# A decode kernel on one core: the key scores of two heads computed by one matmul, with a 4-byte instead of an 8-byte step of the moving operand

## The chip, the cores and the metric

The kernel runs on one core of one Trainium2 chip. The metric is device time in microseconds (us). "Span" is the time from the first to the last instruction of a profiled execution; it is about 1.5 to 3 us shorter than the time of the run. PE is the tensor engine, PEld its weight loads, DVE the vector engine, ACT the scalar engine, and SPq the queue that issues the DMAs.

## The reference, cut to what matters

One token attends to a window of 4096 cached keys in each head. A small dense GELU branch runs beside it, and a gate mixes the two.

```python
Hq, Hkv, Sk, Dh = 32, 16, 32768, 128;  W = 4096;  D = 576;  F = 4608
q = (x @ wq).reshape(B, 1, Hq, Dh).transpose(0, 2, 1, 3)
k = repeat(k_cache[:, :, Sk - W:, :], 2, axis=1)      # 2 query heads per key head
v = repeat(v_cache[:, :, Sk - W:, :], 2, axis=1)
p = softmax(q @ k.T * Dh ** -0.5)
a = (p @ v).reshape(B, 1, Hq * Dh) @ wo
b = gelu(x @ w1 + b1) @ w2 + b2
g = sigmoid((x * gate_w).sum(-1)); return g * a + (1 - g) * b
```

The kernel loads 53.6 MB: 16.8 MB of keys, 16.8 MB of values, and weights. Each byte is used once.

## The kernel before: the parts that matter

The load goes through four large buffers, A to D, which are used again and again. Its order is: w1 (B), wq (A), key tiles 0 to 3 (C, D, B, A), half of w2 (B), value tiles 0 to 3 (C, D, A, C), wo (D), and the rest of w2. So value tile 3 needs the buffer that value tile 0 gives up. That happens only after the softmax and after the matmuls of value tile 0.

A key transfer holds two heads `b` in alternating partitions. The vector engine transposes it as 4-byte words, each word a pair of bf16 (2294 ns for 128 x 2048 words). In the result `kt` the keys of the two heads alternate (`b`), and each word holds two head dimensions (`t`). A score matmul reads one head and one of the two dimensions, so its consecutive columns lie 4 bf16, or 8 bytes, apart (a bank is a piece of 512 fp32 columns of a PSUM tile):

```python
    s_ps = ps_s.tile([P, NCK * 8], FP32, name="s_ps")            # two PSUM banks
    ...
            kv = kt[:].rearrange("p (c e k b t) -> p c e k b t", e=2, b=2, k=16, t=2)
            for u in range(2):
                for b in range(2):
                    for j in range(4):
                        h = h0 + b
                        nc.tensor.matmul(
                            s_ps[:, u * 512 : (u + 1) * 512].rearrange("p (c k) -> p c k", k=16),
                            lhsT=qz[:, h, j, :],
                            rhs=kv[:, u * SL // 2 : (u + 1) * SL // 2, j // 2, :, b, j % 2],
                            ...)
    nc.vector.reduce_max(out=m1[:], in_=s_ps[:], axis=AX.X)
    ...                                       # 8 exps from s_ps (ACT), 2 transposes of p (DVE), sums
    for g in range(NG):
        v_t = big.tile([P, NCK, Dh], BF16, name="v_t", tag="CDAC"[g])
        load(v_t, A_v_cache, g, v_cuts[g])
        ...                                   # 128 matmuls into o_ps
    ...                                       # y_ps += rows of wo and w2, both halves of y in one bank
    out_row = const.tile([64, DH], BF16, name="out_row")
    nc.vector.tensor_copy(out=out_row[0:33, :], in_=y_ps[0:33, :])
    nc.sync.dma_start(out=..., in_=out_row[0:64:32, :])          # two rows
```

## Time and profile before

| | before |
|---|---|
| time, median of 3 runs | 145.44 us (145.25 to 145.54) |
| span | 143.9 us |
| busy: PE / DVE / ACT | 102.9 / 56.5 / 11.9 us |
| DMA, mean over the span | 374 GB/s |

First the strips of the kernel before. Each digit is the busy share, in tenths, of one fortieth of the span (3.6 us); the last line gives GB/s in the same slices.

```profile
PE   0189992718999999999999997740099764384391
DVE  5991003068489858393939102205710000100001
DMA  5999999999999999997999999999404999999930
GB/s 158 421 432 431 412 442 410 412 440 428 424 424 426 428 424 433 403 424 224 415 484 419 437 437 437 437 433 437 182 5 164 415 408 427 431 418 425 402 140 0
```

The DMA is full at about 430 GB/s except for a half-empty slice (65 to 68 us) and a hole of more than two slices (101 to 112 us). PE is solidly busy from the 11th to the 24th slice, which is the scoring of the keys. In that stretch DVE shows gaps (the 3s).

Next, the chain of work that ended last, as the page sums it up: its shares by engine and by line.

```profile
PE 42%; DMA 41%; ACT 7%; DVE 5%; SPq 2%; issue 1%; ACTq 0%
PE s_ps L316 34%; DMA w_t<-in_B_w_dram 21%; DMA k_t<-in_A_k_cache_dram 20%; ACT p_t L354 7%; PE o_ps L398 5%; PE y_ps L178 3%; DVE kt L305 2%; DVE pt L362 2%; SPq L411 1%; DVE m L327 1%; SPq L298 1%; PE t_ps L380 0%; DVE out_row L432 0%; PE mt_ps L329 0%; PE mb_ps L341 0%
```

The longest piece of that chain in order of time (start, length, what):

```profile
40.34 48.52 PE s_ps L316 x112
```

The score matmuls are a third of the chain: 112 of them follow one another without a gap, 48.52 / 112 = 433 ns each. Note that the group list below says 609 ns for one of them. That is from its start to its end, and these overlap; the spacing is what counts for throughput.

The groups of the score matmuls, of the key transposes and of the maximum (busy us, mean ns of one, then idle time of the engine before them and what ended most of it):

```profile
L316 PE MATMUL s_ps<-kt,qz_flat 128*128 128x512 bf16 x128 | 55.6, 609 | 3.6 <-DVE kt L305 3.6
L305 DVE STREAM_TRANSPOSE kt<-k_t 128x2048 f32<-128x2048 f32 x16 | 36.2, 2294 | 12.8 <-PE s_ps L316 9.2
L327 DVE TENSOR_REDUCE m<-s_ps 128x1 f32<-128x1024 f32 x1 | 1.2, 1225 | 9.3 <-PE s_ps L316 9.3
```

PE hardly waits for the transposes (3.6 us), but the transposes wait for PE (9.2 us): PE is the slower of the two. The waits of the DMA queue (us in total, times, longest) tell how this reaches the load:

```profile
SPq L281 <- PE o_ps L398: 23.8, 1, 23.8
...
SPq L370 <- DVE kt L305: 8.2, 1, 8.2
```

Line 281 is the issue of the value tiles. Its longest wait, a single one of 23.8 us, is for the matmuls of value tile 0, which free the buffer for value tile 3. Line 370 is the issue of the first half of w2; it waits for late key transposes. These two waits make the two holes.

Is 433 ns slow for 512 columns? The windows view answers with the granted clock. Columns: window, length, then busy us and count of PE, PEld, DVE, ACT and POOL, granted PE clock, DMA share, GB/s.

```profile
40.00:50.00 10.00, 9.72 (x24) 2.62 (x23) 9.12 (x5) 0.00 (x0) 0.00 (x0) 1.00 1.00 425
130.00:132.00 2.00, 1.35 (x24) 0.96 (x24) 0.00 (x0) 0.00 (x0) 0.00 (x0) 1.00 1.03 432
```

The matmuls of the second stretch, from the timeline:

```profile
130.65 1.63 PE L178 MATMUL y_ps<-wo_t,ov 128*1 128x288 bf16 x24 [1.13 <-DMA wo_t<-in_A_wo_dram]
```

Both stretches read the full clock. In the second, 24 matmuls with 288 contiguous columns take 1.63 us, in pairs that run side by side. The last pair is 0.29 us long, so the pairs are (1.63 - 0.29) / 11 = 122 ns apart: 2.4 columns per ns. The score matmuls manage 512 / 433 = 1.2, which is half.

### The profile page before, as it was taken

The page shows a single profiled execution, that of the slowest core. Times are in us where ns is not written, and L with a number is a line of the kernel's source. Part 1 is how long each engine was busy: PE and PEld are TensorE (multiplying, and loading weights), DVE is VectorE, ACT ScalarE, POOL GpSimd, SP SyncE. Part 2 cuts the span into 40 slices and gives each one's busy share as a digit, 9 for nine tenths or more (in the row PEclk, how much of TensorE's full clock was granted, in tenths as well). Part 3 has the DMA queues.
Part 4 walks back from the last instruction along what each step waited for, and adds up shares of the span by engine and source line. Part 5 has one row for each costly group of instructions (what it writes and reads, how often), then busy time and mean ns, then how long its engine had stood idle before and what let it go on. Part 6 is the DMA issues. An engine that isn't in the chain of part 4 may idle for free.

```text
span 143.9 us, 2461 instructions
## 1 busy us (share of the span) xinstructions
PE 102.9 (72%) x1126; PEld 53.9 (37%) x1126; DVE 56.5 (39%) x81; ACT 11.9 (8%) x21; POOL 0.7 (0%) x6
## 2 busy tenths in 40 slices
PE   0189992718999999999999997740099764384391
PEld 0177992612222222222222221410099763342250
DVE  5991003068489858393939102205710000100001
ACT  3000000010000000000000000499200000000000
POOL 1000000000000000000000000000000000000000
PEclk9999999999999999999999999867555555559959
DMA  5999999999999999997999999999404999999930
GB/s 158 421 432 431 412 442 410 412 440 428 424 424 426 428 424 433 403 424 224 415 484 419 437 437 437 437 433 437 182 5 164 415 408 427 431 418 425 402 140 0
DMA packets 4487, 53.76 MB, mean 374 GB/s; under 512 B 503, under 2 KB 764, under 8 KB 1022
## 3 DMA queue, kind: packets, MB, share of 16 engines
q1 hardware_dynamic: 4468, 53.61, 89.2%
q8 instruction: 8, 0.13, 0.4%
q10 hardware_dynamic: 10, 0.01, 0.0%
q14 instruction: 1, 0.01, 0.0%
HBM read 53.62 MB, written 0.00 MB: 373 GB/s over the span
## 4 chain that ended last, share of the span: by engine, by line
PE 42%; DMA 41%; ACT 7%; DVE 5%; SPq 2%; issue 1%; ACTq 0%
PE s_ps L316 34%; DMA w_t<-in_B_w_dram 21%; DMA k_t<-in_A_k_cache_dram 20%; ACT p_t L354 7%; PE o_ps L398 5%; PE y_ps L178 3%; DVE kt L305 2%; DVE pt L362 2%; SPq L411 1%; DVE m L327 1%; SPq L298 1%; PE t_ps L380 0%; DVE out_row L432 0%; PE mt_ps L329 0%; PE mb_ps L341 0%
## 5 line engine op out<-in xcount | busy, mean ns | idle before, releaser
L316 PE MATMUL s_ps<-kt,qz_flat 128*128 128x512 bf16 x128 | 55.6, 609 | 3.6 <-DVE kt L305 3.6
L305 DVE STREAM_TRANSPOSE kt<-k_t 128x2048 f32<-128x2048 f32 x16 | 36.2, 2294 | 12.8 <-PE s_ps L316 9.2
L316 PEld LDWEIGHTS <-qz_flat 128*128 128x128 bf16 x128 | 14.7, 115 | 43.6 <-issue 42.3
L398 PE MATMUL o_ps<-pt,v_t 128*128 128x8 bf16 x512 | 14.3, 168 | 4.4 <-issue 3.8
L398 PEld LDWEIGHTS <-v_t 128*128 128x128 bf16 x512 | 14.2, 104 | 4.6 <-issue 3.9
L354 ACT ACTIVATE p_t<-s_ps,negm 128x512 bf16<-128x512 f32 x8 | 9.7, 1411 | 60.9 <-DVE negm L345 60.9
L204 PEld LDWEIGHTS <-w_t 128*128 128x128 bf16 x162 | 10.2, 165 | 1.0 <-issue 1.0
L204 PE MATMUL h_ps<-x,w_t 128*128 128x2 bf16 x162 | 10.4, 202 | 0.0
L178 PE MATMUL y_ps<-wo_t,ov 128*1 128x288 bf16 x64 | 5.8, 344 | 4.8 <-DMA wo_t<-in_A_wo_dram 4.8
L178 PE MATMUL y_ps<-w_t,gt 128*1 128x288 bf16 x72 | 7.7, 396 | 2.0 <-DMA w_t<-in_B_w_dram 2.0
L362 DVE STREAM_TRANSPOSE pt<-p_t 128x2048 bf16<-128x2048 bf16 x2 | 4.6, 2311 | 7.4 <-ACT p_t L354 7.4
L416 DVE TENSOR_TENSOR om<-o_ps,rgh 128x128 bf16<-128x128 f32 x1 | 0.3, 292 | 17.8 <-PE o_ps L398 17.8
L380 PE MATMUL t_ps<-ls,ones 128*128 128x32 f32 x2 | 0.6, 396 | 9.1 <-DVE ls L378 9.1
L242 PE MATMUL q_ps<-x,wq_t 128*128 128x2 bf16 x144 | 4.3, 166 | 3.8 <-DMA wq_t<-in_A_wq_dram 3.8
L432 DVE CAST out_row<-y_ps 33x288 bf16<-33x288 f32 x1 | 0.5, 450 | 16.4 <-PE y_ps L178 16.4
L178 PEld LDWEIGHTS <-gt 128*1 128x1 bf16 x72 | 4.2, 111 | 5.0 <-issue 2.2
L178 PEld LDWEIGHTS <-ov 128*1 128x1 bf16 x64 | 3.2, 97 | 7.1 <-issue 4.9
L242 PEld LDWEIGHTS <-wq_t 128*128 128x128 bf16 x144 | 4.1, 104 | 4.0 <-DMA wq_t<-in_A_wq_dram 4.0
L107 PE MATMUL xs_ps<-one_b,rows 1*128 1x1 bf16 x9 | 0.7, 195 | 6.6 <-DVE rows L104 6.6
L327 DVE TENSOR_REDUCE m<-s_ps 128x1 f32<-128x1024 f32 x1 | 1.2, 1225 | 9.3 <-PE s_ps L316 9.3
L380 PEld LDWEIGHTS t_ps<-ls,ones 128*128 128x128 f32 x2 | 0.5, 310 | 9.7 <-issue 9.7
L213 DVE COPY hacc<-h_ps 128x36 f32<-128x36 f32 x1 | 0.2, 196 | 9.7 <-PE h_ps L204 9.7
(66 smaller groups left out, 27.8 us busy)
## 6 DMA issues: line engine op xcount, KB each, us to landing
k_t<-in_A_k_cache_dram SPq DMA_DIRECT2D x6, 2048.0 KB, 31.7
v_t<-in_A_v_cache_dram SPq DMA_DIRECT2D x3, 4096.0 KB, 25.2
w_t<-in_B_w_dram SPq DMA_DIRECT2D x3, 1728.0 KB, 10.5
k_t<-in_A_k_cache_dram SPq DMA_DIRECT2D x4, 1024.0 KB
wo_t<-in_A_wo_dram SPq DMA_DIRECT2D x2, 1728.0 KB
w_t<-in_B_w_dram SPq DMA_DIRECT2D x1, 2592.0 KB
wq_t<-in_A_wq_dram SPq DMA_DIRECT2D x1, 2048.0 KB
v_t<-in_A_v_cache_dram SPq DMA_DIRECT2D x1, 2048.0 KB
```

The source lines that it names most:

```text
L178: nc.tensor.matmul(y_ps[32 * s : 32 * s + 1, :], lhsT=vec, rhs=row[:, s * DH : (s + 1) * DH], start=start, stop=stop, skip_group_check=True,)
L204: nc.tensor.matmul(h_ps[:, j:NF:NJ], lhsT=w1_t[:, i, j:FH:NJ], rhs=x2[:, i, :], start=False, stop=(i == NI - 1 and j == NJ - 1), skip_grou ...
L242: nc.tensor.matmul(q_ps[:, j : Hq : Hq // 2], lhsT=wq_t[:, i, j * Dh : (j + 1) * Dh], rhs=x2[:, i, :], start=(i == 0 and j == 0), stop=(i ...
L298: nc.sync.dma_start(out=k_t[:, f, u * n : (u + 1) * n, :].rearrange("p c d -> p (c d)"), in_=src[:, :, u * n * Dh : (u + 1) * n * Dh],)
L305: nc.vector.transpose(out=kt[:, u * half : (u + 1) * half].bitcast(FP32), in_=k_t[:, f, u * SL // 2 : (u + 1) * SL // 2, :] .rearrange("p ...
L316: nc.tensor.matmul(s_ps[:, u * 512 : (u + 1) * 512].rearrange("p (c k) -> p c k", k=16), lhsT=qz[:, h, j, :], rhs=kv[:, u * SL // 2 : (u + ...
L327: nc.vector.reduce_max(out=m1[:], in_=s_ps[:], axis=AX.X)
L354: nc.scalar.activation(out=p_t[:, cs, :, b], in_=s_ps[:].rearrange("p (c k u) -> p u c k", k=8, u=2)[:, f], func=ACT.Exp, bias=negm[:, b : ...
L362: nc.vector.transpose(out=pt[:, cs, :].rearrange("p c h -> p (c h)"), in_=p_t[:, cs, :, :].rearrange("p c k b -> p (c k b)"),)
L380: nc.tensor.matmul(t_ps[:], lhsT=ones[:], rhs=ls[:], start=True, stop=True)
L398: nc.tensor.matmul(o_ps[:, 8 * g : 8 * g + 8, 0], lhsT=v_t[:, c, :], rhs=pt[:, c, 8 * g : 8 * g + 8], start=(c == 0), stop=(c == NCK - 1),)
L411: nc.sync.dma_start(out=wo_t[:, r0:r1, :], in_=wo_src[:, r0:r1, :])
```

## The change: its intent, and the diff

The change makes the step of the moving operand 4 bytes. To do so it stops selecting a head on the moving side: one matmul takes the keys of both heads, and the stationary operand holds the four query rows of both. Half of the resulting scores are foreign (queries of one head against keys of the other); maximum and exp skip them. The number of matmuls stays at 128 of 512 columns, but the scores now take four PSUM banks instead of two, other tiles move to shared banks, and the maximum reads twice as much. Besides, the output is copied into one row by two engines.

```diff
-    y_ps = ps_y.tile([64, DH], FP32, name="y_ps")
-    nc.vector.memset(y_ps[:], 0.0)
+    y_ps = ps_y.tile([64, 1024], FP32, name="y_ps")
+    y_out = (y_ps[0:1, 0:DH], y_ps[32:33, 512 : 512 + DH])
 ... (h_ps and o_ps move to the shared pool; qz_flat holds 8 pairs of heads instead of 16 heads)
-    s_ps = ps_s.tile([P, NCK * 8], FP32, name="s_ps")
+    s_ps = ps_s.tile([P, SL * 32], FP32, name="s_ps")
 ...
-            kv = kt[:].rearrange("p (c e k b t) -> p c e k b t", e=2, b=2, k=16, t=2)
-            for u in range(2):
-                for b in range(2):
-                    for j in range(4):
-                        h = h0 + b
-                        nc.tensor.matmul(
-                            s_ps[:, u * 512 : (u + 1) * 512].rearrange("p (c k) -> p c k", k=16),
-                            lhsT=qz[:, h, j, :],
-                            rhs=kv[:, u * SL // 2 : (u + 1) * SL // 2, j // 2, :, b, j % 2],
+            kv = kt[:].rearrange("p (c e k t) -> p c e k t", e=2, k=32, t=2)
+            for u in range(4):
+                for j in range(4):
+                    nc.tensor.matmul(
+                        s_ps[:, u * 512 : (u + 1) * 512].rearrange("p (c k) -> p c k", k=32),
+                        lhsT=qz[:, h0 // 2, j, :],
+                        rhs=kv[:, u * SL // 4 : (u + 1) * SL // 4, j // 2, :, j % 2],
 ...
+    m2 = const.tile([P, 2], FP32, name="m2")
+    nc.vector.reduce_max(out=m2[:], in_=s_ps[:].rearrange("p (n b) -> p b n", b=2), axis=AX.X)
+    nc.vector.tensor_tensor(out=m2[:], in0=m2[:], in1=pen2[:], op=ALU.add)
-    nc.vector.reduce_max(out=m1[:], in_=s_ps[:], axis=AX.X)
+    nc.vector.reduce_max(out=m1[:], in_=m2[:], axis=AX.X)
 ...
-                in_=s_ps[:].rearrange("p (c k u) -> p u c k", k=8, u=2)[:, f],
+                in_=s_ps[:].rearrange("p (c k u b) -> p u b c k", k=8, u=2, b=2)[:, f, b % 2],
 ...
-    out_row = const.tile([64, DH], BF16, name="out_row")
-    nc.vector.tensor_copy(out=out_row[0:33, :], in_=y_ps[0:33, :])
-    nc.sync.dma_start(out=..., in_=out_row[0:64:32, :])
+    out_row = const.tile([1, D], BF16, name="out_row")
+    nc.scalar.copy(out=out_row[:, DH:D], in_=y_out[1])
+    nc.vector.tensor_copy(out=out_row[:, 0:DH], in_=y_out[0])
+    nc.sync.dma_start(out=..., in_=out_row[:])
```

More of the change, by code (lines that the diff above doesn't have):

```diff
@@ L57 @@
     ps_y = ctx.enter_context(tc.tile_pool(name="ps_y", bufs=1, space=bass.MemoryType.PSUM))
-    ps_o = ctx.enter_context(tc.tile_pool(name="ps_o", bufs=1, space=bass.MemoryType.PSUM))
-    ps_h = ctx.enter_context(tc.tile_pool(name="ps_h", bufs=1, space=bass.MemoryType.PSUM))
     ps_m = ctx.enter_context(tc.tile_pool(name="ps_m", bufs=2, space=bass.MemoryType.PSUM))
@@ L133 @@
     )
+    pen2 = const.tile([P, 2], FP32, name="pen2")
+    nc.vector.reduce_max(out=pen2[:], in_=pen[:].rearrange("p (a b) -> p b a", b=2), axis=AX.X)
     perm = const.tile([P, 4, 4, 32], BF16, name="perm")
@@ L178, in y_add @@
             nc.tensor.matmul(
-                y_ps[32 * s : 32 * s + 1, :],
+                y_out[s],
                 lhsT=vec,
@@ L187 @@
     y_add(ones[0:1, 0:1], b2g[0:1, :], start=True)
-    h_ps = ps_h.tile([P, NF], FP32, name="h_ps")
+    h_ps = ps_m.tile([P, NF], FP32, name="h_ps", tag="m")
     for j in range(NJ):
@@ L199 @@
         )
-    qz_flat = const.tile([P, Hkv * 514 + 256], BF16, name="qz_flat")
+    qz_flat = const.tile([P, Hkv // 2 * 516 + 128], BF16, name="qz_flat")
     nc.vector.memset(qz_flat[:].bitcast(FP32), 0.0)
@@ L251 @@
     nc.vector.tensor_copy(out=q_b[:], in_=q_ps[:])
-    qj_ps = ps_m.tile([P, 4, Hkv, 2], FP32, name="qj_ps", tag="m")
+    qj_ps = ps_m.tile([P, 4, Hkv // 2, 4], FP32, name="qj_ps", tag="m")
     for j in range(4):
         nc.tensor.matmul(
-            qj_ps[:, j, :, :].rearrange("p h t -> p (h t)"),
+            qj_ps[:, j, :, :].rearrange("p s m -> p (s m)"),
             lhsT=perm[:, j, :, :].rearrange("p b l -> p (b l)"),
@@ L262 @@
         quad = slice(32 * b, 32 * b + 32)
-        diag = qz_flat[quad, 32 * b : 32 * b + Hkv * 514].rearrange("p (h m) -> p h m", m=514)
+        diag = qz_flat[quad, 32 * b : 32 * b + Hkv // 2 * 516].rearrange("p (s m) -> p s m", m=516)
         eng = nc.vector.tensor_copy if b % 2 == 0 else nc.scalar.copy
         eng(
-            out=diag[:, :, 0:512].rearrange("p h (j m) -> p h j m", m=P)[:, :, :, 0:2],
-            in_=qj_ps[quad].rearrange("p j h t -> p h j t"),
+            out=diag[:, :, 0:512].rearrange("p s (j m) -> p s j m", m=P)[:, :, :, 0:4],
+            in_=qj_ps[quad].rearrange("p j s m -> p s j m"),
         )
-    qz = qz_flat[:, 0 : Hkv * 4 * P].rearrange("p (h j m) -> p h j m", h=Hkv, j=4)
+    qz = qz_flat[:, 0 : Hkv // 2 * 4 * P].rearrange("p (s j m) -> p s j m", s=Hkv // 2, j=4)
     def head_rows(cache, g):
@@ L310 @@
                 )
-            kv = kt[:].rearrange("p (c e k b t) -> p c e k b t", e=2, b=2, k=16, t=2)
-            for u in range(2):
-                for b in range(2):
-                    for j in range(4):
-                        h = h0 + b
-                        nc.tensor.matmul(
-                            s_ps[:, u * 512 : (u + 1) * 512].rearrange("p (c k) -> p c k", k=16),
-                            lhsT=qz[:, h, j, :],
-                            rhs=kv[:, u * SL // 2 : (u + 1) * SL // 2, j // 2, :, b, j % 2],
-                            start=(h == 0 and j == 0),
-                            stop=(h == Hkv - 1 and j == 3),
-                            skip_group_check=True,
-                        )
+            kv = kt[:].rearrange("p (c e k t) -> p c e k t", e=2, k=32, t=2)
[5 more added lines that the diff above has]
+                        rhs=kv[:, u * SL // 4 : (u + 1) * SL // 4, j // 2, :, j % 2],
+                        start=(h0 == 0 and j == 0),
+                        stop=(h0 == Hkv - 2 and j == 3),
+                        skip_group_check=True,
+                    )
+    m2 = const.tile([P, 2], FP32, name="m2")
+    nc.vector.reduce_max(out=m2[:], in_=s_ps[:].rearrange("p (n b) -> p b n", b=2), axis=AX.X)
+    nc.vector.tensor_tensor(out=m2[:], in0=m2[:], in1=pen2[:], op=ALU.add)
     m1 = const.tile([P, 1], FP32, name="m1")
-    nc.vector.reduce_max(out=m1[:], in_=s_ps[:], axis=AX.X)
+    nc.vector.reduce_max(out=m1[:], in_=m2[:], axis=AX.X)
     mt_ps = ps_m.tile([1, P], FP32, name="mt_ps", tag="m")
@@ L389 @@
     )
-    o_ps = ps_o.tile([P, Hq, 1], FP32, name="o_ps")
+    o_ps = ps_m.tile([P, Hq, 1], FP32, name="o_ps", tag="m")
     v_cuts = ((NCK,), (NCK,), (NCK,), (64, 32, 32))
@@ L429 @@
         y_add(gt[:, f : f + 1], w2_t[:, f, :], stop=(f == NF - 1))
-    out_row = const.tile([64, DH], BF16, name="out_row")
-    nc.vector.tensor_copy(out=out_row[0:33, :], in_=y_ps[0:33, :])
-    nc.sync.dma_start(
-        out=out.rearrange("a b (s d) -> (a b s) d", s=2), in_=out_row[0:64:32, :]
-    )
+    out_row = const.tile([1, D], BF16, name="out_row")
+    nc.scalar.copy(out=out_row[:, DH:D], in_=y_out[1])
+    nc.vector.tensor_copy(out=out_row[:, 0:DH], in_=y_out[0])
+    nc.sync.dma_start(out=out.rearrange("a b d -> (a b) d"), in_=out_row[:])
 _INS = ['A_x', 'A_k_cache', 'A_v_cache', 'A_wq', 'A_wo', 'B_x', 'B_w1', 'B_b1', 'B_w2', 'B_b2', 'gate_w']
```

## The prediction

> **What bounds the kernel.** The chain that ended last is 42% PE and 41% DMA. 34% of the 143.9 us span is one link: 112 score matmuls (line 316) back to back from 40.34 to 88.86 us, 433 ns each, while the vector engine's K transposes wait 9.2 us for them (group list). The DMA strip is full (about 430 GB/s) but for two holes: half a slice near 65-68 us (w2 waits for a buffer that late transposes free) and 2.2 slices (8 us) at 100-112 us. In the sync queue's waits, v_t waits 23.8 us for o_ps: the fourth V tile needs the first one's buffer, free only after scores, max, exp and the first 128 o_ps matmuls (108 us). So scores delay softmax, and softmax starves DMA.
>
> **What the change moves.**
> - Matmuls stay 128 of 512 columns. Only the step of the moving operand changes: 8 bytes to 4 bytes. At full granted clock (windows view), 433 ns is about 1.18 columns/ns. The 288-column y_ps matmuls at granted clock 1.0 (130-132 us) run at 68 ns each, two side by side, about 2.1 columns/ns, so 433 ns is half rate. I blame the step. [...] In support, w1's weight loads (36-byte step) give 65 ns per pair against 29 ns for contiguous wq. [...] I expect full rate, 512/2.4 = about 216 ns apart [...]: 28 us, not 55.
> - Max reads 2048 instead of 1024 values: 1.2 to about 2.4 us, plus two small operations of 0.15 us.
> - Exp stays 8 x 1.17 us apart[...].
> - Output copy on two engines: 0.45 us to about 0.4. The memsets saved are off the chain.
>
> **On the critical path.** Scores at 8 x 216 = 1.7 us per half tile fall under the transposes (2.3 us) and the DMA (2.45 us per MB). K then ends with its own load, near 67 us; last transpose 69.6, scores end 71.5 (was 88.8). Max until 74.3, exp to about 86, V buffer free near 92, while queued transfers last until about 102. So both holes close and the kernel becomes DMA bound: at 28 us 42.7 MB are still to move, at 0.43 MB/us 99.4 us, end of load about 127.4 (was about 138.2); tail as before, 5.7 us. Span 133; time **134.4 us**, range 132.5 to 138.0. The 17 us saved on scores yield 11.
>
> Chances: faster by over 2% 0.84, within 2% 0.11, slower by over 2% 0.05.
>
> **What the profile would show.** Right: score matmuls 216 ns apart; idle gaps on PE waiting for kt; transposes waiting for DMA, not PE; no hole in the DMA strip from 65 to 112 us; chain mostly DMA plus the y_ps tail; max about 2.5 us. Wrong: spacing still about 430 ns, and the holes stay.
>
> **What would make it wrong.** [...] a 4-byte step is no faster: then about 147 us, 1-2% slower from max and exp. [...]

Passages that no trace or run of this case shows are cut from it: what a line of memory was assumed to allow, a possible cost of exp's step, how the fetch might work, and two risks about the clock. None of them is a term of its sum, which stands whole: 42.7 MB at 0.43 MB per us take 99.4 us, from 28 us on that is 127.4, with the tail of 5.7 us a span of 133, and so 134.4 us. The 2.4 columns per ns behind its 216 ns are the rate of the 288-column matmuls above (122 ns for 288). The 147 us of its last paragraph is the 145.4 us before plus the 1.5 us that it gives for the maximum and the two small operations.

## More of the kernel before

One experiment (e3) is a single execution of unknown state, and only the spacing of its instructions is used.

## The result, and the profile after

The kernel after takes 135.27 us (median of 4 runs, 135.22 to 135.93) against 145.49 us (median of 4, 145.25 to 145.71) before. The ratio is 0.9308, 95% interval 0.9276 to 0.9341. A ratio here is the mean time of one kernel's fast runs over that of the other's fast runs of the same rounds, so it is not quite the ratio of the medians.

| | before | after |
|---|---|---|
| span | 143.9 us | 133.4 us |
| score matmuls, spacing | 433 ns | 217 ns |
| scores end | 88.9 us | 73.5 us |
| value tile 3 issued | 108.4 us | 94.7 us |
| DMA, mean over the span | 374 GB/s | 403 GB/s |

The same strips of the kernel after (a slice is now 3.3 us):

```profile
PE   0239999260957778768789185008923955296771
DVE  6277003118658988988994710663000000100001
DMA  4999999999999999999999999999998999999970
GB/s 137 416 437 419 422 452 400 415 418 442 432 413 437 417 435 418 432 427 405 435 444 474 442 393 418 472 432 393 432 467 373 403 408 441 407 420 422 408 266 0
```

Both holes are gone. The DMA is full from the second slice on until the load ends in the last but one; the lowest slice between, at 100 to 103 us, has 373 GB/s. During the scoring PE now shows mostly 7s and 8s, and DVE 8s and 9s: the roles have changed.

The chain that ended last, by engine:

```profile
DMA 71%; DVE 10%; ACT 7%; PE 6%; issue 2%; SPq 1%; DVEq 0%
```

The groups of the scores and of the transposes:

```profile
L314 PE MATMUL s_ps<-kt,qz_flat 128*128 128x512 bf16 x128 | 31.9, 393 | 11.9 <-DVE kt L305 11.9
L305 DVE STREAM_TRANSPOSE kt<-k_t 128x2048 f32<-128x2048 f32 x16 | 36.0, 2291 | 4.9 <-DMA k_t<-in_A_k_cache_dram 4.7
```

PE's share of the chain fell from 42% to 6%. PE waits 11.9 us for the transposes, and these wait for the load, no longer for PE. In order of time (start, length, engine, line, what, count, idle before), the start of the scoring and a later half tile:

```profile
33.07 5.36 PE L314 MATMUL s_ps<-kt,qz_flat 128*128 128x512 bf16 x16 [3.32 <-DVE kt L305]
...
50.31 1.89 PE L314 MATMUL s_ps<-kt,qz_flat 128*128 128x512 bf16 x8 [0.81 <-DVE kt L305]
...
62.68 8.89 DVE L305 STREAM_TRANSPOSE kt<-k_t 128x2048 f32<-128x2048 f32 x4 [0.41 <-DMA k_t<-in_A_k_cache_dram]
...
71.62 1.90 PE L314 MATMUL s_ps<-kt,qz_flat 128*128 128x512 bf16 x8 [0.30 <-DVE kt L305]
```

Eight matmuls take 1.90 us, of which the last is 0.377 us long, so they are (1.90 - 0.377) / 7 = 217 ns apart. The first sixteen took longer: their weight loads show the first nine about 427 ns apart, after 3.3 us of idle PE. (The kernel before shows no such start: there the spacing is 430 to 434 ns from the second gap of this stage on.) The third row matters below: the last four transposes run back to back from 62.68 to 71.57 us.

The wait of the DMA queue for the buffer of value tile 3:

```profile
SPq L281 <- PE o_ps L400: 11.2, 1, 11.2
```

The maximum over the scores, from the view by tile (least/median/most ns, first and last start):

```profile
L326 DVE TENSOR_REDUCE m<-s_ps x1: 2292/2292/2292, 73.6 to 73.6; 128x2 f32<-128x2048 f32 x1
```

The maximum takes 2.29 us, where it took 1.23. The issue of value tile 3 still waits for the buffer, for 11.2 us, but the strip shows no hole: the queued transfers of tiles 1 and 2 cover the wait. The exps are as far apart as before, 1.18 us.

### The profile page after: what moved, and what is told of

The parts are those of the page before. It is cut to its first block, busy times and chain, and to the rows that moved or that the text cites. A ratio compares the mean times of both kernels' runs of the same rounds, so it can differ in the third digit from the quotient of the medians.

```text
span 133.4 us, 2466 instructions
## 1 busy us (share of the span) xinstructions
PE 81.0 (61%) x1126; PEld 52.5 (39%) x1126; DVE 56.0 (42%) x83; ACT 12.3 (9%) x22; POOL 0.7 (1%) x6
## 4 chain that ended last, share of the span: by engine, by line
DMA 71%; DVE 10%; ACT 7%; PE 6%; issue 2%; SPq 1%; DVEq 0%
DMA k_t<-in_A_k_cache_dram 25%; DMA w_t<-in_B_w_dram 18%; DMA wq_t<-in_A_wq_dram 15%; DMA v_t<-in_A_v_cache_dram 13%; ACT p_t L356 7%; DVE kt L305 5%; PE o_ps L400 3%; DVE pt L364 2%; DVE m L326 2%; PE s_ps L314 1%; SPq L281 1%; PE q_ps L242 1%; PE t_ps L382 0%; PE mb_ps L343 0%; DVE out_row L435 0%
## 5 line engine op out<-in xcount | busy, mean ns | idle before, releaser
L314 PE MATMUL s_ps<-kt,qz_flat 128*128 128x512 bf16 x128 | 31.9, 393 | 11.9 <-DVE kt L305 11.9
L314 PEld LDWEIGHTS <-qz_flat 128*128 128x128 bf16 x128 | 12.7, 99 | 30.7 <-issue 16.8
L400 PE MATMUL o_ps<-pt,v_t 128*128 128x8 bf16 x512 | 14.9, 168 | 7.9 <-DMA v_t<-in_A_v_cache_dram 4.5
L204 PE MATMUL h_ps<-x,w_t 128*128 128x2 bf16 x162 | 10.2, 202 | 0.0
L178 PE MATMUL y_ps<-wo_t,ov 128*1 128x288 bf16 x64 | 7.7, 430 | 3.6 <-DMA wo_t<-in_A_wo_dram 3.6
L178 PE MATMUL y_ps<-w_t,gt 128*1 128x288 bf16 x72 | 7.2, 343 | 1.9 <-DMA w_t<-in_B_w_dram 1.8
L178 PEld LDWEIGHTS <-ov 128*1 128x1 bf16 x64 | 4.0, 119 | 7.1 <-issue 3.6
L178 PEld LDWEIGHTS <-gt 128*1 128x1 bf16 x72 | 3.7, 98 | 4.9 <-issue 2.8
## 6 DMA issues: line engine op xcount, KB each, us to landing
w_t<-in_B_w_dram SPq DMA_DIRECT2D x3, 1728.0 KB, 10.5
```

The source lines that it names most:

```text
L178: nc.tensor.matmul(y_out[s], lhsT=vec, rhs=row[:, s * DH : (s + 1) * DH], start=start, stop=stop, skip_group_check=True,)
L204: nc.tensor.matmul(h_ps[:, j:NF:NJ], lhsT=w1_t[:, i, j:FH:NJ], rhs=x2[:, i, :], start=False, stop=(i == NI - 1 and j == NJ - 1), skip_grou ...
L314: nc.tensor.matmul(s_ps[:, u * 512 : (u + 1) * 512].rearrange("p (c k) -> p c k", k=32), lhsT=qz[:, h0 // 2, j, :], rhs=kv[:, u * SL // 4 ...
L400: nc.tensor.matmul(o_ps[:, 8 * g : 8 * g + 8, 0], lhsT=v_t[:, c, :], rhs=pt[:, c, 8 * g : 8 * g + 8], start=(c == 0), stop=(c == NCK - 1),)
```

## The experiments

Theory: the step of the moving operand alone sets the rate of the score matmuls. Their time is the number of 16-byte lines (blocks of 16 bytes) under their columns, times a constant. The lines were an assumption until e3 measured them. The faster scores then close the holes of the load, and the load is what bounds the kernel after. Rivals: the four banks or the longer runs of 32 columns made the matmuls faster; the other parts of the change made the gain; the softmax still bounds the kernel after.

### e1: the kernel before with the step of 4 bytes alone

```diff
-            kv = kt[:].rearrange("p (c e k b t) -> p c e k b t", e=2, b=2, k=16, t=2)
+            kv = kt[:].rearrange("p (c e b k t) -> p c e k b t", e=2, b=2, k=16, t=2)
```

The matmuls then read the wrong keys. (All runs passed the comparison with the reference, also those that use wrong keys. So that comparison says nothing about the keys; presumably because the softmax over 4096 keys is nearly flat, which was not tested.)

> The kernel before with one edit: the moving operand of the score matmuls is read with a step of 4 bytes instead of 8, in runs of 16 columns as before (its values are then the wrong keys: wrong result on purpose). Step theory: spacing 217 ns instead of 433, both holes of the DMA strip close, about 135.8 us (the after kernel plus 0.5 us for the old output path). Rival, the gain comes from the four PSUM banks or from longer runs of 32 columns: spacing stays at about 433 ns and the time near 145.4. Rival, the gain comes from the other parts of the change: also near 145.4.

Measured: 135.85 us (median of 4) against 145.68 us of the kernel before on the same chip; ratio 0.9329 (0.9295 to 0.9364). The score matmuls of e1 (view by tile: least/median/most ns, first and last start):

```profile
L316 PE MATMUL s_ps<-kt,qz_flat x128: 375/377/629, 33.3 to 73.3; 128*128 128x512 bf16 x128
```

A half tile of e1 in order of time, which gives the spacing, and the DMA strip:

```profile
50.50 1.90 PE L316 MATMUL s_ps<-kt,qz_flat 128*128 128x512 bf16 x8 [0.82 <-DVE kt L305]
```

```profile
DMA  5999999999999999999999999999999999999930
```

The wait of its DMA queue for the buffer of value tile 3:

```profile
SPq L281 <- PE o_ps L398: 9.5, 1, 9.5
```

The spacing is (1.90 - 0.377) / 7 = 217 ns, as after; no hole is left in the strip, and the wait is even shorter than after (9.5 us; 11.2 after, 23.8 before). One edit of the access pattern brings 9.8 us of the 10.2 us. Banks, run length and the rest of the change are not needed for it.

### e2: the kernel after with the step of 8 bytes alone

```diff
-            kv = kt[:].rearrange("p (c e k t) -> p c e k t", e=2, k=32, t=2)
+            kv = kt[:].rearrange("p (c k t) -> p c k t", k=32, t=4)
...
-                        rhs=kv[:, u * SL // 4 : (u + 1) * SL // 4, j // 2, :, j % 2],
+                        rhs=kv[:, u * SL // 4 : (u + 1) * SL // 4, :, j],
```

Wrong keys again.

> The after kernel with one edit: the moving operand is read with a step of 8 bytes, still in runs of 32 columns and into four banks (wrong keys: wrong result on purpose). Step theory: spacing back to 433 ns, the hole before the fourth V tile is back and larger, about 146.4 us: the time before, plus 1.4 us of longer max and small operations, less 0.5 us of output. Rival theories (banks, run length): spacing 217 ns and about 135.3 us.

Measured: 149.04 us; ratio to before 1.0226 (1.0194 to 1.0257). The longest piece of its chain in order of time:

```profile
40.40 50.79 PE s_ps L314 x112
```

Its DMA strip:

```profile
DMA  5999999999999999986999999999102899999960
```

With everything else of the change in place, the step of 8 bytes brings back both holes and the long PE piece. The change without its step is a loss (the whole interval lies above 1, though not above the 2% mark). The size was missed by 2.6 us: the spacing is 50.79 / 112 = 453 ns and not 433, which makes 50.79 - 48.52 = 2.3 us of it. The two patterns touch the same number of lines; this one sweeps whole 256-byte rows, that of the kernel before only half of each. Why that costs 20 ns stays open. (At a step of 4 bytes the half rows of the kernel after gave 217 ns and the whole rows of e3 227.)

### e3: a sweep over steps

Each of the eight key transfers is scored with another step, one evenly stepped pattern of 512 columns (wrong keys).

```diff
-            kv = kt[:].rearrange("p (c e k t) -> p c e k t", e=2, k=32, t=2)
+            st = (1, 2, 3, 4, 5, 6, 8, 16)[h0 // 2]
...
-                        rhs=kv[:, u * SL // 4 : (u + 1) * SL // 4, j // 2, :, j % 2],
+                        rhs=kt[:, j : j + 511 * st + 1 : st].rearrange("p (c k) -> p c k", k=32),
```

> The after kernel, but each of the eight K tiles is scored with another step of the moving operand: 1, 2, 3, 4, 5, 6, 8 and 16 elements of bf16 (2 to 32 bytes), 512 columns in one evenly stepped pattern (wrong result on purpose). If the fetch is limited by 16-byte lines [...]: 217 ns at 2 and 4 bytes, about 320 at 6 (192 lines), 427 at 8, 533 at 10, 640 at 12, 853 at 16 and no more at 32. If the fetch knows only full rate or half rate: 217 or 433 ns and nothing between, also above 8 bytes.

(The times that it expects from 6 to 16 bytes come to 1.67 ns per line, as 427 / 256; that was the author's estimate. The kernel before has 433 / 256 = 1.69.)

Measured from the weight loads, of which each matmul has one. In order of time: the last four loads at 2 bytes, the sixteen at 4 bytes, then two consecutive ones at 6, at 8, at 16 and at 32 bytes. The spacing is the difference of the starts.

```profile
37.91 0.75 PEld L314 LDWEIGHTS <-qz_flat 128*128 128x128 bf16 x4 [0.20 <-issue]
40.28 3.50 PEld L314 LDWEIGHTS <-qz_flat 128*128 128x128 bf16 x16 [1.63 <-issue]
48.32 0.10 PEld L314 LDWEIGHTS <-qz_flat 128*128 128x128 bf16 x1 [0.24 <-issue]
48.66 0.10 PEld L314 LDWEIGHTS <-qz_flat 128*128 128x128 bf16 x1 [0.24 <-issue]
...
54.30 0.12 PEld L314 LDWEIGHTS <-qz_flat 128*128 128x128 bf16 x1 [0.34 <-issue]
54.76 0.11 PEld L314 LDWEIGHTS <-qz_flat 128*128 128x128 bf16 x1 [0.34 <-issue]
...
83.16 0.13 PEld L314 LDWEIGHTS <-qz_flat 128*128 128x128 bf16 x1 [0.77 <-issue]
84.06 0.13 PEld L314 LDWEIGHTS <-qz_flat 128*128 128x128 bf16 x1 [0.77 <-issue]
...
98.59 0.13 PEld L314 LDWEIGHTS <-qz_flat 128*128 128x128 bf16 x1 [0.79 <-issue]
99.50 0.12 PEld L314 LDWEIGHTS <-qz_flat 128*128 128x128 bf16 x1 [0.79 <-issue]
```

Means over the loads of each step (first and last left out where they belong to a neighbour; the 2-byte row uses the last four loads alone, since those before were 427 ns apart at the start of the scoring):

| step, bytes | 16-byte lines under 512 columns | spacing, ns | ns per line |
|---|---|---|---|
| 2 | 64 | 217 | 3.4 |
| 4 | 128 | 227 | 1.77 |
| 6 | 192 | 340 | 1.77 |
| 8 | 256 | 452 | 1.77 |
| 10 | 320 | 564 | 1.76 |
| 12 | 384 | 677 | 1.76 |
| 16 | 512 | 900 | 1.76 |
| 32 | 512 | 918 | 1.79 |

From 4 bytes up the time is the number of 16-byte lines times 1.76 to 1.79 ns, and it stops growing at 16 bytes, where each column has its own line. There is no "full or half rate": 6 bytes lie between. At 2 bytes the columns are the limit (512 / 217 = 2.4 per ns, as in the 288-column matmuls of the kernel before). At 4 bytes the two limits nearly meet, so the change picked the largest of these steps that is nearly free. The expected times came to 1.67 ns per line; the slope was 5% off, the shape was right.

The granted clock fell in the middle of this sweep: it reads 1.00 at 65 to 66 us, in the row of 10 bytes, and 0.50 at 72 to 78 us, in the row of 12 bytes (columns as before):

```profile
65.00:66.00 1.00, 1.00 (x3) 0.23 (x2) 0.00 (x0) 0.00 (x0) 0.00 (x0) 1.00 1.06 445
72.00:78.00 6.00, 6.00 (x10) 1.13 (x9) 0.03 (x1) 0.00 (x0) 0.00 (x0) 0.50 1.03 442
```

The time per line did not change with it (1.76 ns in both rows). So in this run the rate of lines did not follow the granted clock.

### e4 and e8: the kernel after with the old output path

```diff
-    y_ps = ps_y.tile([64, 1024], FP32, name="y_ps")
-    y_out = (y_ps[0:1, 0:DH], y_ps[32:33, 512 : 512 + DH])
+    y_ps = ps_y.tile([64, DH], FP32, name="y_ps")
+    nc.vector.memset(y_ps[:], 0.0)
+    y_out = (y_ps[0:1, :], y_ps[32:33, :])
 ...
-    out_row = const.tile([1, D], BF16, name="out_row")      (and both copies, one-row DMA)
+    out_row = const.tile([64, DH], BF16, name="out_row")    (and one copy, two-row DMA)
```

> The after kernel with the old output path: both halves of y in one PSUM bank with its memset, one copy of 33 partitions by the vector engine, and an output DMA of two rows. The scores keep their step of 4 bytes. From the traces, last y matmul to the end of the span took 3.2 us before and 2.7 after, so I expect 0.5 us more than after: about 135.8 us. If the two-engine copy is worth nothing: 135.3.

Measured: 136.08 us, ratio to before 0.9332 (0.9305 to 0.9360). The kernel after was not in those rounds, so both were run again side by side, five rounds each:

> The after kernel unchanged, to stand on the same chip and in the same rounds as the old-output kernel beside it: 135.3 us.

> The after kernel with the old output path once more, now beside the after kernel itself. From the traces the old path ends 3.1 us after the last y matmul and the new one 2.7 us: 0.4 us slower than the after kernel, about 135.7. If equal within 0.1 us, the new output path is worth nothing.

Measured: after 135.59 us, old output 135.89 us (medians of 6); ratios to before 0.9294 (0.9256 to 0.9332) and 0.9312 (0.9274 to 0.9349). The difference of 0.3 us has the expected sign but the intervals overlap. The traces agree with the sign: from the last y matmul to the end of the span it is 3.1 to 3.3 us in all four profiles with the old path (before, e1, e4, e8) and 2.7 us in all five with the new one (after, e2, e5, e6, e7). The new output path is worth some tenths at most; more was not settled.

### e5 and e6: the softmax made longer

Four (e5) or all eight (e6) of the exps are done twice, with the same result.

```diff
-        for b in range(HB):
+        for b in (0, 0, 1, 1, 2, 2, 3, 3) if f == 0 else range(HB):      # e5
+        for b in (0, 0, 1, 1, 2, 2, 3, 3):                               # e6
```

> The after kernel with the four exps of the first half each done twice (same result), which delays the softmax by 4 x 1.175 = 4.7 us. Theory: the after kernel is bound by its load and its softmax has some slack. In its trace the third V tile has landed at 102.9 us and stopped moving perhaps 1.4 us earlier, the fourth is issued at 94.7 and needs about 2 us to start: an estimate of 4.8 us of slack. So within 0.5 us of the after kernel, about 135.3 to 135.8. Rival, the softmax is still on the critical path as the chain of waits of the after kernel suggests (exp and max are links of it): 4.7 us more, about 140.0.

> The after kernel with all eight exps done twice (same result): the softmax is delayed by 8 x 1.175 = 9.4 us. Slack theory with 4.8 us of slack: about 4.6 us more than the after kernel, near 139.9, with a hole in the DMA strip before the fourth V tile. No slack: 9.4 us more, near 144.7. Slack of 10 us, as the prediction had it: no change.

Two terms of the 4.8 us can be read from the trace of the kernel before, where value tiles 2 and 3 stand apart (columns as before):

```profile
103.00:103.50 0.50, 0.00 (x0) 0.00 (x0) 0.50 (x1) 0.00 (x0) 0.00 (x0) 0.50 0.16 66
103.50:104.00 0.50, 0.00 (x0) 0.00 (x0) 0.47 (x3) 0.00 (x0) 0.00 (x0) 0.50 0.00 0
...
108.00:109.00 1.00, 1.00 (x43) 1.00 (x41) 0.00 (x0) 0.00 (x0) 0.00 (x0) 0.50 0.00 0
109.00:110.00 1.00, 1.00 (x44) 1.00 (x42) 0.00 (x0) 0.00 (x0) 0.00 (x0) 0.50 0.65 131
110.00:111.00 1.00, 1.00 (x43) 1.00 (x41) 0.00 (x0) 0.00 (x0) 0.00 (x0) 0.50 0.49 197
111.00:112.00 1.00, 1.00 (x44) 1.00 (x42) 0.00 (x0) 0.00 (x0) 0.00 (x0) 0.50 1.07 459
```

Tile 2 landed at 104.8 us (issued at 79.6, 25.2 us to landing), and its traffic stopped between 103.0 and 103.5: 1.3 to 1.8 us earlier (1.4 in the estimate). Tile 3 was issued at 108.35 us and full traffic began at 111. Less what was moved by then, (131 + 197) / 430 = 0.76 us, that is a start of 1.9 us (2 in the estimate).

Measured: 137.09 us (e5) and 142.91 us (e6), against 135.59 us of the kernel after on the same chip: 1.5 and 7.3 us more. The delays were larger than I had set, as the issues of value tile 3 show (start, length; one line each from after, e5 and e6):

```profile
94.66 1.83 SPq L281 DMA_DIRECT2D v_t<-in_A_v_cache_dram  x3
```

```profile
100.72 2.18 SPq L281 DMA_DIRECT2D v_t<-in_A_v_cache_dram  x3
```

```profile
106.46 1.83 SPq L281 DMA_DIRECT2D v_t<-in_A_v_cache_dram  x3
```

They came 6.1 and 11.8 us later than after. (In e7, on the same chip as e5 and e6, the issue came at 94.72 us, so the baseline is good to 0.1 us. The doubled exps ran 1.31 us apart on average, not 1.18, and a doubled half took 10.5 us.) Slack is delay less cost: 6.1 - 1.5 = 4.6 us and 11.8 - 7.3 = 4.5 us. The two agree, and agree with the estimate of 4.8 us. The windows of e5 and then of e6 (columns as before; the last is GB/s) show the queue running dry soon after 100 us in both, whatever the softmax does, and when it fills again:

```profile
98.00:100.00 2.00, 2.00 (x81) 2.00 (x79) 0.02 (x1) 0.00 (x0) 0.00 (x0) 0.50 1.14 492
100.00:102.00 2.00, 2.00 (x81) 2.00 (x79) 0.00 (x0) 0.00 (x0) 0.00 (x0) 0.50 0.27 107
102.00:104.00 2.00, 2.00 (x76) 1.96 (x74) 0.00 (x0) 0.00 (x0) 0.00 (x0) 0.50 0.80 287
```

```profile
100.00:102.00 2.00, 0.00 (x0) 0.00 (x0) 2.00 (x2) 0.00 (x0) 0.00 (x0) 0.50 0.35 147
102.00:104.00 2.00, 1.57 (x45) 1.60 (x46) 0.90 (x4) 0.00 (x0) 0.00 (x0) 0.50 0.00 0
104.00:106.00 2.00, 2.00 (x82) 2.00 (x79) 0.00 (x0) 0.00 (x0) 0.00 (x0) 0.50 0.03 8
106.00:108.00 2.00, 2.00 (x82) 2.00 (x79) 0.00 (x0) 0.00 (x0) 0.00 (x0) 0.50 0.34 66
```

So the kernel after is bound by its load, and maximum, exp and the transposes of p have 4.5 us to spare. The chain of the kernel after passes through the exps (7%) all the same. It follows what released what, and value tile 3 was released by the softmax; that the DMA engines were busy with other tiles meanwhile it doesn't show. The DMA strip does.

None of these runs beats the kernel after. e1 (135.85 us, with wrong keys) and e8 (135.89 us) come closest. With a full load there are only the ends left: the first slice and the last 4.6 us.

## Why the prediction was right, point by point

- **The step as the cause: right.** e1 and e2 move the step alone and move the time with it; e3 shows how the time grows with it, from 227 ns at 4 bytes to 900 at 16. Spacing 217 ns against 216 predicted.
- **16-byte lines: an assumption before, measured by e3.** From 4 bytes up each line takes 1.76 to 1.79 ns, and the time stops growing at 16 bytes (900 ns, and 918 at 32). Two columns per line (8 bytes) halve the rate of the matmul (433 ns); four (4 bytes) give all or nearly all of it (217 to 227 ns), and between them only 6 bytes was measured (340 ns). The supporting evidence, weight loads with a step of 36 bytes, was slightly off in its figures: from the trace of the kernel before, 108 pairs in 6.86 us less the last one's 0.20 give 62 ns, and 48 contiguous pairs in 1.42 us less 0.17 give 27 ns (I had 65 and 29). No experiment varied the weights' step.
- **Both holes close, the kernel becomes bound by its load: right** (strip after; e5, e6).
- **The slack: mis-sized.** I had the buffer free at 92 us and the queue dry at 102, so 10 us of slack. It was 94.7 us, and the queue ran dry just after 100, leaving 4.5 us with the start of a transfer. Two of the 2.7 us came from the transposes: I let the last one start when the last key landed (67 us). But the transfer before the last one, of 2 MB, must have landed whole (62.55 us) before its two transposes start (62.68 us), so DVE runs one transpose behind, and the last four ran back to back until 71.6 us instead of 69.6. From there to the end of the exps nothing was lost (87.8 us against about 86). The rest came after the exps: the transpose of p, the sums and the matmuls of value tile 0 took 6.8 us, where I had about 6. None of it shows in the time, because of the slack.
- **End of load and tail: two small errors that cancel.** Load to 127.4 us predicted; the last slice with traffic (126.7 to 130.0 us, 266 GB/s, or 2.1 us at 420) puts it at about 128.8. The tail was 4.6 us, not 5.7. Before, the load ended in the slice from 136.7 us with 140 GB/s, so about 137.9, and the tail was 6.0. In this profiled run the last y matmuls came in two bursts, the first of them 18 in 1.27 us; before, 36 came in one burst of 4.04 us. When the same kernel was profiled again (e7), 36 came in one burst of 3.76 us and the span was 133.7 us, so this varies from run to run and is worth some tenths. The granted clock differed too: 1.00 in both bursts of the profiled run, 0.50 from 137 to 140 us in the burst before. The output path gives another 0.5 us (3.2 to 2.7 us after the last y matmul). The rest was not looked into. The load ended 1.4 us later than predicted and the tail was 1.1 us shorter, so that the span was met to 0.4 us is partly luck. Span 133.0 predicted, 133.4 measured; time 134.4 and 135.27.
- **Maximum and exp: right.** 2.29 us (2.4 predicted), exp unchanged at 1.18 us although its step in PSUM doubled to 16 bytes.
- **Output: small, as predicted,** and not settled beyond that.
- **17 us earlier scores yield 11: nearly.** Scores ended 15.4 us earlier and the time fell by 10.2.

## What to carry to other kernels

Read the spacing of matmuls and not their duration, and where it is twice what the columns need (here 2.4 columns per ns in the 288-column matmuls and 1.2 in the scores), look at the step of the moving operand: in these runs bf16 columns 4 bytes apart ran at full rate (217 ns for 512), 8 bytes apart at half (433 ns). It can pay to compute results that nobody reads (here half of the scores) if that makes the operand denser. And where a late result holds back the buffer of a later transfer, the gain ends where the load has no hole left: measure the slack by making the slow stage longer.
